# Gate and up of two row blocks made together by seven half products, and two turns moved to TensorE

## The chip, the core and the metric

The kernel runs on one core of one Trainium2 chip. A core has a matrix engine (TensorE, PE in the profile, with its weight loads as PEld), a vector engine (VectorE, DVE), a scalar engine (ScalarE, ACT), a general engine (GpSimd, POOL) and a queue engine (SyncE, SP) that here issues every transfer between DRAM and the on-chip memory. PE writes into eight banks of 128 x 512 floats; DVE and ACT read them. The metric is the time of one execution in microseconds of device time.

## The reference

One pre-norm transformer block on 2048 rows of 640 numbers, in float32.

```python
def _A_ref(x, wqkv, wo):          # H = 32 heads of 20, window W = 8, dilation 2
    qkv = (x @ wqkv).reshape(B, S, 3, H, Dh) ...
    idx = pos[:, None] - off[None, :]          # each row looks at 8 rows, 2 apart
    logits = einsum("bhsd,bhswd->bhsw", q, k[idx]) * scale
    o = einsum("bhsw,bhswd->bhsd", softmax(logits), v[idx])
    return o.reshape(B, S, D) @ wo

def _B_ref(x, w_gate, w_up, w_down):           # 640 -> 1728 -> 640
    return (_silu(x @ w_gate) * (x @ w_up)) @ w_down

h  = x + _A_ref(_layernorm(x), wqkv, wo)
h2 = h + _B_ref(_layernorm(h), w_gate, w_up, w_down)
```

## The kernel before

**Tiles.** The 2048 rows are four blocks (0 to 3) of 512; a block lies on 128 partitions as four row groups j. The 640 columns are five chunks of 128 (c = 0 to 4). The 1728 hidden columns are 14 tiles (0 to 13) of 128, the last of 64. Attention runs on DVE by block and by four head groups of 8 heads.

**Three passes.** A float32 number is kept as a rounded high half and the rest, a low half. ACT casts the high half and DVE subtracts to get the low one. A product is three passes: high x high, high x low, low x high. So gate and up of one tile in one block are 2 x 5 chunks x 3 passes = 30 matmuls (`proj`, L756), into banks 5 and 6; ACT then makes the SiLU of the gate's bank (L787), DVE multiplies it with the up bank (L788), and ACT and DVE split the result (L789, L791). The down product (`down`, L768) adds it into banks 0 to 4, five banks x 3 passes = 15 matmuls a tile. `finish` turns bank 4 with four transposes (L813) and adds the banks to the residual rows.

**Stages on PE.** First the qkv products of all blocks (`qkv`, L515), then the output projection of block 0 (`wo`, L686) and its norm; then, for each block, 14 tiles of gate, up and down, with the next block's output projection and norm strewn in between (bank 7). Attention on DVE runs beside all of this until block 2's tiles, and its results go over DRAM (`osc`) back as columns, in four transfers per half block and head group.

**The norm between the projection and gate/up.** Its rows have to be turned into columns. Block 0 does so on PE (`x_columns`, five times four transposes, L408, with high half on ACT L411 and low half on DVE L412). Blocks 1 and 2 turn half by DVE and DRAM and half on PE (`pair_columns`). Block 3 turns all rows by DVE and DRAM (`turn_rows`, `turned_back`, `turned_columns`), since it is in `TURN`.

**Weights.** `load_ffn` brings a tile's gate, up and down weights (960 KB, L732) into one of two raw buffers. In block 0 the low halves are made on DVE (L750) and stored in DRAM (`lsc`); blocks 1 and 2 load them from there (`LOADED`, L738); block 3 makes them again on DVE.

**What sets the order.** The functions only add operations to a plan, with the ranges that each reads and writes, an assumed cost and a priority. `Plan.order` places them by a list schedule on the five engines (smaller priority number first among those that are ready), shifts a few operations by a table that is keyed by an operation's number (`SHIFT`), and writes the program out in that order. Each engine then runs its own queue strictly in order; a wait in front of an instruction holds all that is behind it, on SP too.

Of the kernel before, what the change touches and what calls it, by code (L numbers as in the profile page):

```python
# [23 lines left out]
NF = 14  # L24
KEPT = range(NF)
LOADED = (1, 2)
TURN = (3,)
# [7 lines left out]
PR = {'x': 4, 'yst': 8, 'yld': 6, 'wqd': 1.5, 'wqh': 8, 'wql': 2.5, 'qev': 0.5, 'kvs': 4, 'atl': 0.9, 'exp': 0.9, 'ost': 0.9, 'wod': 4, 'woh': 8, 'wol': 2.5, 'old': 1, 'fld': 2.5, 'lst': 10, 'wev': 2.5, 'fh': 1.2, 'fl': 0.5, 'ln1': 10, 't1': 3, 'wo0': 0.4, 'wo': 2, 'ln1t': 8, 'xb': 0.4, 'tr': 1.2, 't1t': 6, 'ln1d': 1.5, 'hst': 1, 'hld': 6, 'ht': 3, 'hc': 0.4}  # L35
# [111 lines left out]
tt = dve  # L147
# [10 lines left out]
def program(tc, x_in, wqkv_in, wo_in, ffn_in, ffl_in, const_in, out):  # L158
# [7 lines left out]
    with tc.tile_pool(name="sb", bufs=1) as sb, tc.tile_pool(  # L166
# [6 lines left out]

        def sha_t():
            if "sha" not in late:
                late["sha"] = sb.tile([128, 5120], F32R, name="sha", tag="sha")
            return late["sha"]

        def h_t():
            if "h" not in late:  # L180
                late["h"] = sb.tile([128, 5120], F32, name="h", tag="sha")
            return late["h"]
# [19 lines left out]
        zsc = dr.tile([NB, D, 4, 64], F32, name="zsc")  # L202
        lsc = dr.tile([NF, 128, 1920], F32, name="lsc")
# [58 lines left out]
        class LnStats:  # L262
# [41 lines left out]
            def apply_pair(self, j):  # L304
                o = lambda: f(XN, 1280).rearrange("p (f j t) -> p f j t", j=2, t=32)[:, :, j, :]
                P.add("ACT", 0.95, lambda: A.activation(o(), self.src(j).rearrange("p (f t) -> p f t", t=32), AF.Identity, bias=f(self.NB + j, 1), scale=f(self.RS + j, 1)),
                      r=[self.srcr(j), rf(self.NB + j, 1), rf(self.RS + j, 1)], w=[rf(XN, 1280)], prio=self.prio)

# [273 lines left out]

        def att_av(b, g, n, ko, vo, qo, lo, mo):
# [7 lines left out]
            for jp in range(2):  # L591
# [11 lines left out]
                for m in (4, 2):  # L603
                    P.add("DVE", tt(320 * m), lambda m=m, half=half: half(m, lambda v: v[:, :, 0:m, :]),
                          r=[rf(PROD, 2560)], w=[rf(PROD, 2560)], prio=20)
                P.add("DVE", tt(320), lambda half=half: half(1, lambda v: v[:, :, 0:1, :]), r=[rf(PROD, 2560)], w=[rf(PROD, 2560)], prio=20)
# [26 lines left out]
        def hsl(b, j, o=0, n=640):  # L633
            s = 2560 * (b % 2) + 640 * j + o
            return s, s + n

        wn = [0]
        ln = [0]

        def wo(b, prio, bks):  # L640
# [16 lines left out]
            stats = LnStats(b, lambda j: h_t()[:, slice(*hsl(b, j))], lambda j: ("sha",) + hsl(b, j), prio, turned=b in TURN)  # L657
            h0 = 2560 * (b % 2)
            if b:
                P.add("SP", 0.6, lambda: Q.dma_start(h_t()[:, h0 : h0 + 2560], x_in[b].rearrange("p j c -> p (j c)")),  # L660
                      w=[("sha", h0, h0 + 2560)], prio=PR["old"], nbytes=nb(512, 2560))
            for j in range(NJ):
# [3 lines left out]
                for i in range(3) if j % 2 == 0 else ():  # L666
# [11 lines left out]
                for half in range(2):  # L678
# [10 lines left out]
                    P.add("ACT", act(320), lambda bk=bk, xo=xo: A.copy(f(xo, 320), banks[bk][:, 0:320]), r=[pb(bk)], w=[rf(xo, 320)], prio=PR["wev"])  # L689
                lo, hi = hsl(b, j)  # L690
                if b:
                    P.add("DVE", dve(640), lambda lo=lo, hi=hi, j=j: V.tensor_add(h_t()[:, lo:hi], h_t()[:, lo:hi], f(XN + 640 * j, 640)),
                          r=[rf(XN + 640 * j, 640), ("sha", lo, hi)], w=[("sha", lo, hi)], prio=prio)
                else:
                    xr = XR + 640 * (j % 2)
                    P.add("SP", 0.45, lambda j=j, xr=xr: Q.dma_start(f(xr, 640), x_in[0, :, j, :]), w=[rf(xr, 640)], prio=PR["old"], nbytes=nb(128, 2560))
                    P.add("DVE", dve(640), lambda lo=lo, hi=hi, j=j, xr=xr: V.tensor_add(h_t()[:, lo:hi], f(xr, 640), f(XN + 640 * j, 640)),
                          r=[rf(XN + 640 * j, 640), rf(xr, 640)], w=[("sha", 0, 5120) if j == 0 else ("sha", lo, hi)], prio=prio)
                stats.one(j)
# [9 lines left out]
                if b == 0 and j >= NJ - 2:  # L709
# [4 lines left out]
            if b and b not in HALF:  # L714
# [45 lines left out]
        def down(i, ao, dn, k):  # L760
            first, last = i == 0, i == NF - 1
            passes = ((0, 0), (0, 1)) if last else ((0, 0), (1, 0), (0, 1))
# [187 lines left out]
```

## Time and profile before

| | us |
|---|---|
| median of the three runs shown | 860.32 |
| lowest and highest | 858.07, 860.82 |
| the profiled execution, its own time | 857.67 |
| its span | 855.9 |

The profile has one execution. Its page lists busy times by engine, then the span in 40 slices of 21.4 us, where a digit is the busy share in tenths. A list of waits says who waited for whom: the total, how often, the longest. Rows in order of time give the start, the length, the engine, the line, the operation, what it writes and reads, and the number of instructions merged in the row; in brackets stands the idle time before it and what ended it. The end of a matmul is modelled and reaches into the next one, so distances are taken from start to start.

In the trace, block 1's tiles begin at 399.11 us, block 2's at 556.87 us and block 3's at 713.38 us; attention's last row on DVE begins at 614.31 us; PE's last matmul ends at about 852.3 us.

### The profile page before, as it was taken

The numbers are of one execution on the slowest core, as the hardware profiler recorded it, in microseconds if no ns is written. First come the engines' busy times: TensorE is split into PE (matmuls) and PEld (weight loads), VectorE is DVE, ScalarE is ACT, GpSimd is POOL, SyncE is SP. The second block draws the span as 40 slices with busy tenths as digits, with TensorE's granted clock in tenths as the row PEclk, the third lists the DMA queues.
The fourth block names the chain that finished last, engine by engine and source line by source line (L and its number), as shares of the span: only waits on it lengthen the run. The fifth ranks groups of instructions, "written<-read, shape, count | busy, mean of one in ns | idle before, by whom it ended". The sixth has DMA issues, their size and how long they took to land.

```text
span 855.9 us, 10646 instructions
## 1 busy us (share of the span) xinstructions
PE 848.7 (99%) x3987; PEld 721.3 (84%) x3987; DVE 658.4 (77%) x781; ACT 395.7 (46%) x637; POOL 2.5 (0%) x10
## 2 busy tenths in 40 slices
PE   9999999999999999999999999999999999999998
PEld 7888888889878888988888898888888888888886
DVE  7799999999999999999999998999622326333332
ACT  7571463434763334666434468444355534333321
POOL 0000000000000000000000000000000000000000
PEclk9999999999999999999999999999999999999999
DMA  8998697579786969398999976897552755222301
GB/s 285 278 296 252 199 275 205 155 212 293 235 265 243 291 223 311 128 242 276 316 309 322 287 233 205 241 360 273 180 204 94 227 203 200 92 93 93 105 18 62
DMA packets 87732, 187.90 MB, mean 220 GB/s; under 512 B 34289, under 2 KB 51185, under 8 KB 86913
## 3 DMA queue, kind: packets, MB, share of 16 engines
q1 hardware_dynamic: 87680, 187.23, 68.6%
q8 instruction: 31, 0.51, 0.2%
q14 instruction: 21, 0.16, 0.1%
HBM read 142.23 MB, written 44.96 MB: 219 GB/s over the span
## 4 chain that ended last, share of the span: by engine, by line
PE 71%; DVE 18%; DMA 6%; issue 3%; ACT 1%; SPq 0%; DVEq 0%; ACTq 0%
PE bank L756 43%; PE bank L768 22%; PE bank L686 6%; DVE fa L594 4%; DVE fa L602 4%; DVE fa L563 2%; DVE fa L568 2%; DMA fa<-in_x_dram 1%; DMA fa<-qsc 1%; DMA qsc<-st 1%; DVE ra L491 1%; DMA osc<-fa 1%; DVE fa L316 1%; DVE fa L609 1%; DMA fa<-in_const_dram 1%
## 5 line engine op out<-in xcount | busy, mean ns | idle before, releaser
L756 PE MATMUL bank<-shb,ra 128*128 128x512 f32 x1620 | 379.7, 390 | 1.3 <-DVE shb L412 1.3
L756 PEld LDWEIGHTS bank<-shb,ra 128*128 128x128 f32 x1620 | 303.1, 188 | 63.5 <-ACT shb L411 1.5
L768 PE MATMUL bank<-ra,acts 128*128 128x512 f32 x656 | 160.6, 390 | 0.0
L768 PEld LDWEIGHTS bank<-ra,acts 128*128 128x128 f32 x656 | 122.5, 188 | 25.0
L788 DVE TENSOR_TENSOR fa<-bank,fa 128x512 f32<-128x512 f32 x52 | 35.9, 690 | 113.4 <-PE bank L756 113.0
L515 PE MATMUL bank<-ra,sha 128*128 128x480 f32 x480 | 106.1, 380 | 0.5 <-ACT sha L478 0.3
L515 PE MATMUL bank<-ra,shb 128*128 128x480 f32 x470 | 102.9, 378 | 0.1
L515 PEld LDWEIGHTS bank<-ra,sha 128*128 128x128 f32 x480 | 89.8, 188 | 14.4 <-ACT sha L478 0.6
L515 PEld LDWEIGHTS bank<-ra,shb 128*128 128x128 f32 x470 | 88.0, 188 | 13.6 <-DVE shb L398 0.4
L733 ACT CAST ra<-fa 128x1280 fp32r<-128x1280 f32 (+1 forms) x56 | 68.9, 1230 | 58.7 <-PE bank L756 58.5
L594 DVE TENSOR_TENSOR fa<-fa 128x1280 f32<-128x1280 f32 x64 | 93.6, 1488 | 1.0
L563 DVE TENSOR_TENSOR fa<-fa 128x2560 f32<-128x2560 f32 x32 | 90.3, 2821 | 1.8 <-DMA fa<-qsc 1.4
L602 DVE TENSOR_TENSOR fa<-fa 128x1280 f32<-128x1280 f32 (+2 forms) x96 | 89.7, 934 | 2.5
L568 DVE TENSOR_REDUCE fa<-fa 128x128 f32<-128x2560 f32 x32 | 90.0, 2814 | 0.4
L787 ACT ACTIVATE fa<-bank 128x512 f32<-128x512 f32 x52 | 31.1, 599 | 104.9 <-PE bank L756 101.3
L750 DVE TENSOR_TENSOR ra<-fa,ra 128x640 fp32r<-128x640 f32 (+1 forms) x82 | 64.6, 818 | 18.1 <-ACT ra L734 18.0
L520 ACT ACTIVATE st<-bank,fa 128x480 f32<-128x480 f32 x64 | 42.0, 658 | 76.4 <-PE bank L515 74.8
L686 PE MATMUL bank<-ra 128*128 128x320 f32 x480 | 74.8, 309 | 0.5 <-DVE ra L676 0.5
L686 PEld LDWEIGHTS bank<-ra 128*128 128x128 f32 x480 | 72.4, 188 | 2.8 <-DVE ra L676 0.7
L734 ACT CAST ra<-fa 128x640 fp32r<-128x640 f32 x56 | 40.8, 730 | 59.6 <-PE bank L768 59.6
L789 ACT CAST acts<-fa 128x512 fp32r<-128x512 f32 x52 | 32.2, 619 | 43.1 <-DVE fa L788 40.4
L768 PE MATMUL bank<-acts,ra 128*128 128x512 f32 x164 | 46.2, 390 | 0.0
(101 smaller groups left out, 487.7 us busy)
## 6 DMA issues: line engine op xcount, KB each, us to landing
fa<-in_ffn_dram SPq DMA_DIRECT2D x52, 960.0 KB, 6.6
ra<-lsc SPq DMA_DIRECT2D x26, 640.0 KB, 5.6
fa<-ksc SPq DMA_DIRECT2D x32, 440.0 KB, 5.9
fa<-vsc SPq DMA_DIRECT2D x32, 440.0 KB, 6.6
ra<-lsc SPq DMA_DIRECT2D x30, 320.0 KB, 4.9
lsc<-ra SPq DMA_DIRECT2D x13, 640.0 KB, 5.7
ksc<-st SPq DMA_DIRECT2D x32, 160.0 KB, 3.9
qsc<-st SPq DMA_DIRECT2D x16, 320.0 KB, 5.0
```

Source lines behind the costliest of these rows:

```text
L515: T.matmul(banks[bk][:, 0:480], l, r_(wq(g, w, c), 480), start=(p, c) == first_mm, stop=(p, c) == last_mm)
L520: P.add("ACT", act(480) + 0.06, lambda bk=bk, j=j: A.activation(stage_t()[:, so : so + 1920].rearrange("p (t j c) -> p t j c", t=3, j=NJ)[ ...
L563: P.add("DVE", dve(2560), lambda: V.tensor_tensor(f(PROD, 2560).rearrange("p (j w c) -> p j w c", j=2, w=W), window(ko, 2 * jp), f(qo + 32 ...
L568: P.add("DVE", dve(2560), lambda: V.tensor_reduce(f(lo + 128 * jp, 128), f(PROD, 2560).rearrange("p (n d) -> p n d", d=DH), axis=AX.X, op= ...
L594: V.tensor_tensor(f(PROD + 1280 * jj, 1280).rearrange("p (w h d) -> p w h d", w=W, d=DH), f(vo + 160 * j, 1280).rearrange("p (w h d) -> p ...
L602: V.tensor_add(dst(v), v[:, :, 0:m, :], v[:, :, m : 2 * m, :])
L686: T.matmul(banks[bk][:, 0:320], l, r_(m, 320), start=p == 0 and c == 0, stop=p == 2 and c == NC - 1)
L733: P.add("ACT", act(n), lambda: A.copy(r_(gu, n), f(raw, n)), r=[rf(raw, n)], w=[rr(gu, n)], prio=PR["fh"])
L734: P.add("ACT", act(640), lambda: A.copy(r_(dn[0], 640), f(raw + n, 640)), r=[rf(raw + n, 640)], w=[rr(dn[0], 640)], prio=PR["fh"])
L750: P.add(eng, c, lambda o=o: E.tensor_sub(ra[p0:, lo + o : lo + o + 640], fa[p0:, raw + o : raw + o + 640], ra[p0:, hi + o : hi + o + 640]. ...
L756: T.matmul(banks[bk], r_(gu + 1280 * w + wid * c + col, 128), x2(a, c), start=p == 0 and c == 0, stop=p == 2 and c == NC - 1)
L768: T.matmul(banks[k], l, m, start=first and p == 0, stop=last and p == len(passes) - 1)
```

## The change

**Seven half products.** Take tiles p and p + 6 (p = 0 to 5) as one pair, and blocks 2 and 3. Of the five chunks, 0 and 1 are one half of the columns and 2 and 3 the other; chunk 4 is done plainly. With A11, A12 the halves of block 2's normed columns, A21, A22 those of block 3, and B11, B21 the weights of tile p, B12, B22 those of tile p + 6, the four products of block and tile are made by Winograd's form of Strassen's scheme, from column sums S1 = A21 + A22, S2 = S1 - A11, S3 = A11 - A21, S4 = A12 - S2 and weight sums T1 = B12 - B11, T2 = B22 - T1, T3 = B22 - B12, T4 = B21 - T2 (the last with its sign turned):

- A11 B11 and A12 B21 are made early (`early`), as part of block 2's tile p, which is then finished as before. The first of the two is copied from its bank by ACT before the second is added, and stored in DRAM (`msc`), for gate and for up.
- S2 T2, S1 T1, S3 T3, A22 T4 and S4 B22 are made later (`pair`), for gate and up, on banks 5, 6 and 7. The running sums are read from a bank by DVE while its accumulation goes on.
- A pair gives tile p and tile p + 6 of block 3 at once, and tile p + 6 of block 2, whose gated product is kept in on-chip memory; its down products run at the very end (`closing`).

So the order of stages behind block 1 is: tiles 12 and 13 of block 2, six early tiles, the output projection and norm of block 3, tiles 12 and 13 of block 3, six pairs, block 3's rows out, six closing down products for block 2, its rows out. The column sums are made once by DVE and ACT (`column_combinations`), the weight sums for each pair (`combo`).

**Turns.** The norm of block 3 is turned on PE (20 transposes) as block 0's, its statistics are made on DVE, and ACT keeps the sorted columns in float32 too, since the sums need them. The last head group of block 3 is no longer turned by DVE and sent over DRAM: PE turns it (two times four transposes, `last_columns`), and only the three groups before it come from DRAM. Block 2's down sum is added to its rows in two parts, so `finish` turns a bank once more (four transposes).

Some priorities change too. The table of shifts keeps its numbers, which count operations, so from the first added operation on they mean other ones. Parts of the diff that only rename or resize buffers are left out below.

```diff
-TURN = (3,)
+TURN = ()
...
+        def last_columns(jp, at, col, sorted_, prio):
...
+            def tr():
+                for jj in range(2):
+                    for t, s in ((0, -96), (1, 32)):
+                        T.transpose(banks[bk][:, 256 * jj + 128 * t : 256 * jj + 128 * t + 128], f(last_rows(2 * jp + jj) + s, 128), ident)
...
+        def product(bk, terms, start, stop):
+            for p, (w, a) in enumerate(((0, 0), (0, 1), (1, 0))):
...
+        def early(p):
...
+            load_ffn(2, p, gu, dn)
+            ws = lambda c, col: (gu + 256 * c + col, gu + 1280 + 256 * c + col)
+            both = ((5, 0), (6, 128))
+            for n, (bk, col) in enumerate(both):
+                product(bk, [(ws(0, col), x2, (0, 1), shr)], True, False)
+                P.add("ACT", act(512), lambda n=n, bk=bk: A.copy(f(EB[n], 512), banks[bk]), ...)
+                P.add("SP", 0.45, lambda n=n: Q.dma_start(msc[p, n], f(EB[n], 512)), ...)
+            for bk, col in both:
+                product(bk, [(ws(2, col), x2, (2, 3, 4), shr)], False, True)
+            gate(p, ao, so, JG)
...
+        def pair(p):
+            lo_, hi_ = RAW, RAW + 1920
...
+            t1 = combo(1, 0, B12, B11)
+            t2 = combo(0, 1, B22, t(0))
+            t3 = combo(2, 2, B22, B12)
+            t4 = combo(3, 3, B21, t(1))
...
+            X, Y = (5, 7), (6, 5)
+            def add(h, bk, src, dst):
+                dv(0, lambda: V.tensor_add(fb(h, dst), banks[bk], fb(h, src)), ...)
+            def sum_of(h, part):
+                if part == 0:
+                    product(X[h], [(t2(C[h]), c2, (0, 1), c2r)], True, False)
+                    add(h, X[h], 0, 1)
+                elif part == 1:
+                    product(Y[h], [(t1(C[h]), c1, (0, 1), c1r), (kws(1, C[h]), x3, (4,), x3r)], True, False)
+                elif part == 2:
+                    product(X[h], [(t3(C[h]), c3, (0, 1), c3r)], False, False)
+                    add(h, X[h], 0, 2)
+                elif part == 3:
+                    product(X[h], [(t4(C[h]), x3, (2, 3), x3r), (kws(0, C[h]), x3, (4,), x3r)], False, True)
+                    add(h, X[h], 0, 0)
+                elif part == 4:
+                    add(h, Y[h], 2, 2)
+                else:
+                    product(Y[h], [(b22(C[h]), c4, (0, 1), c4r), (kws(1, C[h]), ck, (0,), ckr)], False, True)
+                    add(h, Y[h], 1, 1)
+            for n, (h, part) in enumerate(((0, 0), (0, 1), (1, 0), (0, 2), (0, 4), (1, 2), (0, 3), (1, 3), (0, 5), (1, 1), (1, 4), (1, 5))):
...
-        for b in range(NB):
-            if b + 1 < NB:
-                wo(b + 1, PR["wo"], (7,))
...
+        for b in range(2):
+            wo(b + 1, PR["wo"], (7,))
             do_down = ffn(b)
-            if b + 1 < NB:
-                ln2_columns(b + 1, 1)
+            ln2_columns(b + 1, 1)
             do_down()
             finish(b)
...
+        for i in range(2 * NP, NF):
+            step(plain(i, x2, shr))
+        for p in range(NP):
+            step(early(p), 2 if p == NP - 1 else 1)
+        wo(3, PR["w3"], (7,))
+        ln2_columns(3, 1)
...
+        finish(2, store=False)
+        column_combinations()
...
+        for i in range(2 * NP, NF):
+            step(plain(i, x3, x3r))
+        for p in range(NP):
+            for t in pair(p):
+                step(t)
+        downs([pend.pop(0)], False, True)
+        finish(3)
...
+        downs(todo, False, True, fb)
+        finish(2, fb, final=True)
```

How the queues change is shown at three places. In these rows bank_73, 74 and 75 are banks 5, 6 and 7, and bank_68 to 72 banks 0 to 4.

PE's queue before, one tile of block 2 or 3 in its steady state: gate, up, then the down product of the tile before (L756 is `proj`, L768 `down`).

```order
L756 MATMUL bank_73<-shb,ra 128x512 x15
L756 MATMUL bank_74<-shb,ra 128x512 x15
L768 MATMUL bank_72<-acts,ra 128x512 x3
L768 MATMUL bank_68<-ra,acts 128x512 x3
L768 MATMUL bank_69<-ra,acts 128x512 x3
L768 MATMUL bank_70<-ra,acts 128x512 x3
L768 MATMUL bank_71<-ra,acts 128x512 x3
```

PE's queue now, one pair (L932 is `product`, L857 `down`); in the order of the rows: S2 T2 of the gate, S1 T1 of the gate, S2 T2 of up, S3 T3 of the gate and of up, A22 T4 of the gate and of up, S4 B22 of the gate, S1 T1 of up, down products, S4 B22 of up.

```order
L932 MATMUL bank_73<-ra 128x512 x6
L932 MATMUL bank_74<-ra 128x512 x9
L932 MATMUL bank_75<-ra 128x512 x6
L932 MATMUL bank_73<-shb,ra 128x512 x6
L932 MATMUL bank_75<-shb,ra 128x512 x6
L932 MATMUL bank_73<-ra 128x512 x9
L932 MATMUL bank_75<-ra 128x512 x9
L932 MATMUL bank_74<-shb,ra 128x512 x9
L932 MATMUL bank_73<-ra 128x512 x9
L857 MATMUL bank_72<-acts,ra 128x512 x3
L857 MATMUL bank_68<-ra,acts 128x512 x3
L932 MATMUL bank_73<-shb,ra 128x512 x9
```

Two products on the same bank now stand 6 matmuls apart at three points (bank 5 from its S3 T3 to its A22 T4, bank 7 from its S2 T2 to its S3 T3, bank 5 from up's S1 T1 to its S4 B22), with a read by DVE between; before, a bank's next product stood 30 matmuls on.

DVE's queue now, from the start of the column sums to tile 13's gated product (L993 to L1000 the sums, L992 their low halves, L872, L876, L883 and L878 the gated products of block 3's tiles 12 and 13 and their low halves).

```order
L993 TENSOR_TENSOR fa<-fa 128x1024
L995 TENSOR_TENSOR fa<-fa,shb 128x1024
L996 TENSOR_TENSOR fa<-fa,shb 128x1024
L998 TENSOR_TENSOR fa<-shb,fa 128x1024
L872 TENSOR_TENSOR fa<-bank_74,fa 128x512
L992 TENSOR_TENSOR ra<-fa,ra 128x1024
L883 TENSOR_TENSOR acts<-fa,acts 128x512
L992 TENSOR_TENSOR ra<-fa,ra 128x1024
L999 TENSOR_TENSOR fa<-fa,shb 128x1024
L876 TENSOR_TENSOR fa<-bank_73,fa 64x512
L1000 TENSOR_TENSOR fa<-shb,fa 128x1024
L878 TENSOR_TENSOR acts<-fa,acts 64x512
```

Behind these come the last two sums, the four weight sums of pair 0, their low halves, and the first two reads of pair 0's banks, before the low half of S3.

SP's queue now, around the first weights of pair 0 (L1024 the two raw tiles, L1018 the low half of down weights, L828 low halves of block 3's tiles 12 and 13, L970 and L1028 the stored products out and in).

```order
L822 DMA fa<-in_ffl_dram 128x1280
L1028 DMA fa<-msc 128x512
L828 DMA ra<-lsc 128x1280
L970 DMA msc<-fa 128x512 x2
L1018 DMA ra<-lsc 128x640
L828 DMA ra<-lsc 128x640
L1024 DMA fa<-in_ffn_dram 128x1920
L828 DMA ra<-lsc 128x640 x2
L1024 DMA fa<-in_ffn_dram 128x1920
```

The L828 row ahead of the first raw tile goes into a place that the down weights of the last early tile hold, so the raw tile is issued when that tile's down products are done.

More of the change, by code (lines that the diff above doesn't have):

```diff
@@ L172, in program, with __init__, __getitem__, two @@
         late = {}
+        class Two:
+            def __init__(self, *t):
+                self.t = t
+            def __getitem__(self, at):
+                o = 2560 * (at[1].start >= 2560)
+                return self.t[o // 2560][:, at[1].start - o : at[1].stop - o]
+        def two(name, dtype):
+            if name not in late:
+                late[name] = Two(*(sb.tile([128, 2560], dtype, name=f"{name}{i}", tag=f"sha{i}") for i in range(2)))
+            return late[name]
         def sha_t():
[L175 to L177 removed]
+            return two("sha", F32R)
         def h_t():
[L180 to L182 removed]
+            return two("h", F32)
+        def upper(name, dtype):
+            if name not in late:
+                late[name] = sb.tile([128, 2560], dtype, name=name, tag="sha1")
+            return late[name]
         def stage_t():
@@ L665, in wo @@
                 jp = j // 2
-                for i in range(3) if j % 2 == 0 else ():
+                if b == 3 and j % 2 == 0:
+                    last_columns(jp, at, col, sorted_, prio)
+                for i in range(3) if j % 2 == 0 and b < 3 else ():
                     c, n = 2 * i, 1 if i == 2 else 2
@@ L767, in down, with downs @@
                     l, m = act_t()[:, ao + 512 * a + 128 * k : ao + 512 * a + 128 * k + 128], r_(dn[w], 512)
-                T.matmul(banks[k], l, m, start=first and p == 0, stop=last and p == len(passes) - 1)
+                T.matmul(banks[bk], l, m, start=first and p == 0, stop=last and p == len(passes) - 1)
+        DB = (0, 1, 2, 3, 4)
+        def downs(batch, first, last, db=DB):
+            for k in (4, 0, 1, 2, 3):
+                P.add("PE", sum(3 if t[0] < NF - 1 else 2 for t in batch) * 0.229,
+                      lambda k=k: [down(*t, k, first and n == 0, last and n == len(batch) - 1, db[k]) for n, t in enumerate(batch)],
+                      r=[x for i, ao, dn in batch for x in (("ab", ao, ao + 1024), rr(dn[0], 640), rr(dn[1], 640))], w=[pb(db[k])], prio=10)
@@ L770, in ffn, with halves, do_down @@
+        def halves(src, srcr, ao, prio=0, lprio=0):
+            P.add("ACT", act(512), lambda: A.copy(act_t()[:, ao : ao + 512], src()), r=srcr, w=[("ab", ao, ao + 512)], prio=prio)
+            P.add("DVE", dve(512), lambda: V.tensor_sub(act_t()[:, ao + 512 : ao + 1024], src(), act_t()[:, ao : ao + 512].bitcast(F32)),
+                  r=srcr + [("ab", ao, ao + 512)], w=[("ab", ao + 512, ao + 1024)], prio=lprio)
         def ffn(b):
             pend = []
-            def do_down(count=1):
-                batch = [pend.pop(0) for _ in range(count)]
-                for k in (4, 0, 1, 2, 3):
-                    P.add("PE", sum(3 if t[0] < NF - 1 else 2 for t in batch) * 0.229,
-                          lambda k=k: [down(i, ao, dn, k) for i, ao, dn in batch],
-                          r=[x for i, ao, dn in batch for x in (("ab", ao, ao + 1024), rr(dn[0], 640), rr(dn[1], 640))], w=[pb(k)], prio=10)
+            def do_down():
+                t = pend.pop(0)
+                downs([t], t[0] == 0, t[0] == NF - 1)
@@ L821, in finish @@
                     if j == 0:
[L822 to L825 removed]
+                        keys = [hrow(b, k, 512, 128)[1] for k in range(NJ)]
```

326 lines of the change are left out of this document (273 added, 53 removed).

## The prediction

> **What bounds the kernel now.** I read the page's busy times, slices and chain first, then what the matmul engine waited for, then its rows in order of time.
>
> ```profile
> span 855.9 us, 10646 instructions
> PE 848.7 (99%) x3987; PEld 721.3 (84%) x3987; DVE 658.4 (77%) x781; ACT 395.7 (46%) x637; POOL 2.5 (0%) x10
> PE   9999999999999999999999999999999999999998
> DVE  7799999999999999999999998999622326333332
> PEclk9999999999999999999999999999999999999999
> PE 71%; DVE 18%; DMA 6%; issue 3%; ACT 1%; SPq 0%; DVEq 0%; ACTq 0%
> ```
>
> TensorE (PE) is busy in every slice; VectorE (DVE) is full for the first two thirds only, and in the last stage has more than half its time free:
>
> ```profile
> 697.00:856.00 159.00, 155.33 (x690) 128.26 (x688) 61.96 (x89) 50.62 (x67) 0.63 (x1) 1.00 0.27 95
> ```
>
> (a row of the windows: stretch, length, busy time of PE, weight loads, DVE, ACT and POOL, granted clock, DMA's share, GB/s). The waits of PE, added up, say how little a better order could still give:
>
> ```profile
> PE bank L423 <- POOL ra L842: 1.3, 1, 1.3
> PE bank L756 <- DVE shb L412: 1.3, 1, 1.3
> PE bank L686 <- DVE ra L676: 0.5, 1, 0.5
> PE bank L515 <- ACT sha L478: 0.3, 1, 0.3
> PE bank L515 <- ACT ra L489: 0.2, 1, 0.2
> ```
>
> That is 3.6 us in 855.9. So the time is the number of matmuls by what each takes, and a matmul taken out is time taken out, until something makes PE wait. What one takes is read from the distance between rows in order of time, since the last matmul of a row overlaps the next row:
>
> ```profile
> 533.87 0.60 PE L373 MATMUL bank<-fa 128*128 128x128 f32 x4
> 534.23 2.33 PE L768 MATMUL bank<-ra,acts 128*128 128x512 f32 x9
> 556.87 13.80 PE L756 MATMUL bank<-shb,ra 128*128 128x512 f32 x60
> 594.31 6.96 PE L756 MATMUL bank<-shb,ra 128*128 128x512 f32 x30
> 601.11 0.84 PE L768 MATMUL bank<-acts,ra 128*128 128x512 f32 x3
> 628.31 2.36 PE L686 MATMUL bank<-ra 128*128 128x320 f32 x15
> 630.50 1.32 PE L756 MATMUL bank<-shb,ra 128*128 128x512 f32 x5
> ```
>
> Thirty matmuls of 512 columns take 601.11 - 594.31 = 6.80 us, 0.2267 us each; four transposes of 128x128 take 0.36 us, 0.09 each; fifteen of the output projection's 320-column matmuls 2.19 us. Block 2's feed-forward part starts at 556.87 us, and up to there PE's queue stays as it was but for two or three pieces moved by a few places.
>
> **Matmuls out and in.** A pair of column tiles in two blocks was 2 x 2 x 2 (gate, up) x 5 chunks x 3 passes = 120 matmuls. Now the early part has 30, and the seven half products' rest 2 x (2 + 3 + 2 + 3 + 3) x 3 = 78, so 108: twelve fewer in each of six pairs, 72, at 0.2267 us: **-16.3 us**. Added are 32 transposes: 20 for block 3's norm, 8 for the last head group, 4 because block 2's down sum is now turned and added twice: 32 x 0.09 = **+2.9 us**. Nothing else on PE changes in number. What is left is where PE waits.
>
> By the Trainium skill (TensorE: Matmul & The Clock Gate, section on the clock gate) a warm matmul comes every N / 2.4 GHz + 2.5 ns, 215.7 ns at 512 columns, by which the 72 would be 15.5 us. The trace's 226.7 is used.
>
> **Place 1: block 3's norm comes back through PE.** Before, it was turned by DVE and DRAM, far from PE. Now the last row group's chain (copy, sum, statistics, root, scale, transposes, halves) ends directly before the first block-3 tile. The nearest row is block 0, which does the same already:
>
> ```profile
> 239.01 1.04 PE L408 MATMUL bank<-fa 128*128 128x128 f32 x8
> 239.77 1.06 ACT L411 CAST shb<-bank 128x512 fp32r<-128x512 f32 x2
> 240.49 1.88 DVE L412 TENSOR_TENSOR shb<-bank,shb 128x512 fp32r<-128x512 f32 x3
> 241.32 13.85 PE L756 MATMUL bank<-shb,ra 128*128 128x512 f32 x60 [1.27 <-DVE shb L412]
> ```
>
> PE stood 1.27 us after its transposes. Between the last transposes and the first block-3 product there are now three down matmuls (0.7 us) as cover, and two more casts on ScalarE (ACT) ahead (the sorted copies of the norm, 0.6 each). These cancel about: **+1.3 us**; bounds 0 and 3.
>
> **Place 2: from the first block-3 tile to the first pair's third half product.** This is the dearest term. Here DVE makes the four combinations of normed columns and the four of weights, and PE has only tiles 12 and 13 of block 3 to do meanwhile. DVE's rates:
>
> ```profile
> 557.75 1.87 DVE L820 TENSOR_TENSOR h<-bank,h 128x512 f32<-128x512 f32 x3
> 573.39 2.89 DVE L594 TENSOR_TENSOR fa<-fa 128x1280 f32<-128x1280 f32 x2
> 590.91 0.84 PE L768 MATMUL bank<-acts,ra 128*128 128x512 f32 x3
> 591.18 0.69 DVE L788 TENSOR_TENSOR fa<-bank,fa 128x512 f32<-128x512 f32 x1 [1.12 <-PE bank L756]
> 591.78 2.81 DVE L568 TENSOR_REDUCE fa<-fa 128x128 f32<-128x2560 f32 x1
> ```
>
> 512 elements alone take 0.69 us but follow each other every 0.60; 1280 every 1.40, so 1024 some 1.13 (on the line between). From the last low half of block 3's columns to the low half of the third combination (first read in pair 0's third half product) DVE's queue holds 10 operations of 1024 and 17 of 512: 11.3 + 10.2 = 21.5 us, 23.9 if none overlaps. PE's queue has 88 matmuls between the same points: 19.9 us. So PE waits 1.6 to 4.0 us even if DVE never does. DVE will wait once: its queue is strict, and the gated product of tile 12 stands in it behind ACT's SiLU, which stands behind two casts of pair 0's weights. Their transfer is queued on SP behind a load into tile 13's slot that the last early tile's down matmuls hold, and so starts about when the first block-3 tile does:
>
> ```profile
> fa<-in_ffn_dram SPq DMA_DIRECT2D x11, 960.0 KB, 6.3
> fa<-in_ffn_dram SPq DMA_DIRECT2D x11, 960.0 KB, 4.7
> 243.27 1.28 ACT L787 ACT_TABLE_LOAD   x1
> ```
>
> (before's windows 560 to 700 and 700 to 850 us). Landing at 4.7 to 6.3, two casts 1.1, table load 1.3, SiLU 0.6: 7.7 to 9.3 us after the tile's start, where DVE would otherwise have come to that product at about 7 (30 matmuls 6.8, and 0.27 from PE to DVE as in the rows at 590.91 and 591.18). Late by 0.7 to 2.3. Together 2.3 to 6.3; I take **+4.5 us**, above the middle because each late operand also holds matmuls that the next one waits for.
>
> **Place 3: inside the pairs.** A running sum is read from its bank and the next half product is added onto the same bank, with 6 matmuls in between at three points of a pair: 6 x 0.2267 = 1.36 us. The trip is 0.27 (PE's next row to DVE's start) + 0.69 + some 0.15 back (an estimate, half of the 0.27) = 1.1 us. It fits when DVE is free, and in the order it is at two of the three; at the third (before up's last product) two 512-operations run ahead and still end in time. DVE has 21 such operations in a pair, 12.6 to 14.5 us of its 108 x 0.2267 = 24.5. Taken as **0**; if one more DVE operation (0.60) stands ahead at each point, 0.34 us x 18 = 6.2 us.
>
> The Trainium skill (Perfetto Trace Analysis, Optimizing Tensor Performance, Matmuls) says that matmul groups should rotate through banks so that one's evacuation overlaps the next's matmuls, which these sums do over three banks only; it is the rule behind the second rival below.
>
> **Place 4: small ones.** PE must find the last attention group's columns ready at the output projection of block 3: 253 matmuls and four transposes after 556.87, plus nine more, 616.6 us. Attention's last DVE rows in this trace:
>
> ```profile
> 613.79 0.49 DVE L602 TENSOR_TENSOR fa<-fa 128x320 f32<-128x320 f32 x1
> 614.31 0.51 DVE L609 STREAM_TRANSPOSE fa<-fa 128x320 f32<-128x320 f32 x1
> ```
>
> The last transpose goes, and three column halves (0.60 + 0.60 + 0.35) come ahead and two (0.8) behind: about 616 us, half a microsecond before PE asks. The early tiles' bank copies on ACT (0.60 and the two trips, 1.0 us, under 1.36 or, once, 0.68) two gated products asked for early, and one pass in block 1 that now comes 12 matmuls sooner and so meets the read of its bank, cost some tenths each. **+1.0 us**, bounds 0 and 3.
>
> **Place 5: transfers in the pairs.** Both raw weight tiles have one buffer each. The second is free after the pair's second product and a copy (some 5.6 us into the pair), and its next use is DVE's first combination for the next pair, some 13 us in, with 0.8 us of further slack before a matmul is late: 8 us for a transfer that took 4.7 to 6.6. **0**; the other end is the first rival's.
>
> **Sum** on the profiled execution (857.67 us, of them 855.9 span): -16.3 + 2.9 + 1.3 + 4.5 + 1.0 = -6.6, so 851.1. The median of the runs shown, 860.32, is 2.65 above that execution, so **853.7 us** as the runs go.
>
> **Rivals.**
> (a) Late weights, the other side. Each pair's combinations stand in DVE's strict queue ahead of the reads that free the banks, so a tile landing after its 8 us holds PE one for one, in five pair changes. For it: 3.7 MB (raw tiles 1.97, low halves and stored products 1.70) go through one queue in each pair, in strict order behind its waits, and one kind took longer than that where the queue was full:
>
> ```profile
> out_dram<-h SPq DMA_DIRECT2D x2, 320.0 KB, 11.8
> ```
>
> Against it: in the last stage DMA was busy 27% at 95 GB/s, and a pair asks for 150 GB/s (3.7 MB in 24.5 us). With landing at 11.8: 5 x 3.8 = 19 us, 872.7. It decides from 8 + 6.6 / 5 = 9.3 us on.
> (b) Bank trips exposed: Place 3's 6.2 us and Place 2's upper end (+1.8): 853.7 + 8.0 = 861.7, no measurable change. For it: PE issues in strict order and nothing else can fill in. Against: the three operations ahead of each read are counted above. If a wait passed some 3.4 us, by the Trainium skill (the same TensorE page and section) the clock would halve for such a window, +1.7 us; here the granted clock stayed at 1.00 with waits up to 1.3.
> (c) Full gain: the waits of Places 1, 2 and 4 vanish under what PE has queued: -13.4, 846.9. Against: DVE's 21.5 us against 19.9 is a count.
>
> **How the numbers follow.** Forecast 0.62, (c) 0.14, (b) 0.13, (a) 0.11. About 0.3% (2.6 us) is what a measurement here tells from no change. Forecast and (c), with a little of (b)'s lower part, are faster: 0.78. The rest of (b): same, 0.11. (a): slower, 0.11. The range runs from (c), 847, to 861: Places 1, 2 and 4 at their ends give -6.6 + 5.5 = -1.1, 859.2, and most of (b) is taken in.
>
> **What would show it.** In the changed kernel PE's 512-column matmuls number 2379 and the transposes 128. Steady pairs should be 24.5 us apart, with no PE wait over 0.3 us in them (Place 3, 5). PE's waits should sit between the last transposes and the first pair, on DVE's combinations and gated products, 4 to 8 us in all. It is wrong if the pairs are 26 us apart or more (a, b), if that stretch costs under 2 or over 10 us, or if PE waits for the last attention columns by more than 2 us.

## The result, and the profile after

| | before | changed |
|---|---|---|
| median of four runs beside each other, us | 860.13 | 851.73 |
| lowest and highest | 858.07, 860.82 | 851.40, 852.59 |
| the profiled execution, its time and span | 857.67, 855.9 | 851.40, 849.6 |

The ratio is 0.9908 (95% interval 0.9889 to 0.9927), and 0.9924 (0.9911 to 0.9938) in a second set of runs: about 0.8 to 0.9% faster. The prediction was 853.7 us, within 847 to 861; on the profiled execution it was -6.6 us, and -6.3 came. The median came 2.0 us lower than predicted because the 2.65 us between profiled execution and median, taken over from the kernel before, were not there: the changed kernel's median lies 0.3 us above its profiled execution.

The page of the changed kernel: span, busy times of TensorE and of VectorE, the 40 slices of VectorE, the granted clock of TensorE (in tenths of full speed; 9 is 90% or more).

```profile
span 849.6 us, 10832 instructions
PE 839.5 (99%) x3947; PEld 709.9 (84%) x3947; DVE 719.4 (85%) x892; ACT 403.3 (47%) x669; POOL 1.9 (0%) x9
DVE  7799999999999999999999899999945986555652
PEclk9999999999999999999999999999999999999999
```

PE is as full as before over a shorter span. DVE is nearly full once more in the two slices from 658 to 701 us (9 and 8 tenths), where the column sums are made, and then about half busy to the last slice but one, where it mostly had a third or less. From the list of PE's waits, longest in total first:

```profile
...
PE bank L857 <- DVE acts L878: 0.9, 2, 0.8
PE bank L932 <- ACT ra L1048: 0.9, 1, 0.9
...
PE bank L932 <- DVE shb L992: 0.3, 1, 0.3
PE bank L846 <- DVE fa L872: 0.2, 1, 0.2
PE bank L846 <- ACT fa L871: 0.2, 1, 0.2
```

These five were not there before: tile 13's low half (L878, in block 2 and in block 3), the cast of a weight sum (L1048), the low half of a column sum (L992), and two short ones in block 1 (L871, L872). A bank read of the pairs (L1070) or a transfer is not among them. The pairs themselves, in order of time (start, length, operation, number of matmuls): the first rows of pairs 2, 3 and 4.

```profile
722.95 4.92 PE L932 MATMUL bank<-ra 128*128 128x512 f32 x21
...
747.43 4.92 PE L932 MATMUL bank<-ra 128*128 128x512 f32 x21
...
771.91 4.92 PE L932 MATMUL bank<-ra 128*128 128x512 f32 x21
```

They are 24.48 us apart, as is pair 5 from pair 4: 108 x 0.2267 = 24.48. What was lost was lost between block 3's first tile and pair 1, which begins at 698.47:

```profile
658.23 10.49 PE L954 MATMUL bank<-ra 128*128 128x512 f32 x45
...
672.89 0.74 PE L857 MATMUL bank<-acts,ra 128*128 128x512 f32 x2 [0.77 <-DVE acts L878]
...
676.34 5.08 PE L932 MATMUL bank<-ra 128*128 128x512 f32 x21 [0.85 <-ACT ra L1048]
...
682.14 2.56 PE L932 MATMUL bank<-shb,ra 128*128 128x512 f32 x10 [0.27 <-DVE shb L992]
```

698.47 - 658.23 = 40.24 us for 163 matmuls, which are 36.95: **3.3 us**. These 40.24 us are called the stretch below. Up to the wait in the third half product, for which 4.5 us were predicted, it is 682.14 - 658.23 = 23.91 us for 93 matmuls, which are 21.08: 2.8 us. The prediction's forecast of 4 to 8 us of waiting between the last transposes and the first pair was too high. A second loss lies where only some tenths had been costed, in block 1. Its first tile begins at 399.37 us, block 2's at 558.16: 158.79 us, where the kernel before took 157.76 (399.11 to 556.87).

### The profile page after: what moved, and what is told of

Same layout as the page of the kernel before. It is cut to its first block, busy times and chain, and to the rows that moved or that the text cites. A ratio compares the mean times of both kernels' runs of the same rounds, so it can differ in the third digit from the quotient of the medians.

```text
span 849.6 us, 10832 instructions
## 1 busy us (share of the span) xinstructions
PE 839.5 (99%) x3947; PEld 709.9 (84%) x3947; DVE 719.4 (85%) x892; ACT 403.3 (47%) x669; POOL 1.9 (0%) x9
## 5 line engine op out<-in xcount | busy, mean ns | idle before, releaser
L846 PE MATMUL bank<-shb,ra 128*128 128x512 f32 x810 | 191.3, 390 | 1.7 <-DVE shb L441 1.3
L846 PEld LDWEIGHTS bank<-shb,ra 128*128 128x128 f32 x810 | 151.2, 188 | 33.5 <-ACT shb L440 1.5
L857 PE MATMUL bank<-ra,acts 128*128 128x512 f32 x656 | 162.8, 391 | 0.0
L857 PEld LDWEIGHTS bank<-ra,acts 128*128 128x128 f32 x656 | 122.1, 188 | 24.7
L932 PE MATMUL bank<-shb,ra 128*128 128x512 f32 x360 | 87.6, 391 | 0.3 <-DVE shb L992 0.3
L932 PEld LDWEIGHTS bank<-shb,ra 128*128 128x128 f32 x360 | 67.0, 188 | 15.2 <-ACT fa L969 0.7
L1070 DVE TENSOR_TENSOR fa<-bank,fa 128x512 f32<-128x512 f32 x60 | 41.1, 691 | 44.3 <-PE bank L932 43.2
L776 PEld LDWEIGHTS bank<-ra 128*128 128x128 f32 x480 | 72.0, 188 | 3.8 <-ACT fa L779 1.0
L932 PE MATMUL bank<-ra 128*128 128x512 f32 x288 | 68.5, 390 | 0.9 <-ACT ra L1048 0.9
L932 PEld LDWEIGHTS bank<-ra 128*128 128x128 f32 x288 | 53.9, 188 | 12.9 <-ACT ra L1048 1.3
L823 ACT CAST ra<-fa 128x1280 fp32r<-128x1280 f32 (+1 forms) x38 | 46.0, 1211 | 28.6 <-PE bank L846 23.5
L882 ACT CAST acts<-fa 128x512 fp32r<-128x512 f32 x47 | 29.2, 620 | 50.1 <-DVE fa L1100 22.9
```

Of the source, the lines that this page charges most:

```text
L776: T.matmul(banks[bk][:, 0:320], l, r_(m, 320), start=p == 0 and c == 0, stop=p == 2 and c == NC - 1)
L823: P.add("ACT", act(n), lambda: A.copy(r_(gu, n), f(raw, n)), r=[rf(raw, n)], w=[rr(gu, n)], prio=PR["fh"])
L846: T.matmul(banks[bk], r_(gu + 1280 * w + wid * c + col, 128), x2(a, c), start=p == 0 and c == 0, stop=p == 2 and c == NC - 1)
L857: T.matmul(banks[bk], l, m, start=first and p == 0, stop=last and p == len(passes) - 1)
L932: T.matmul(banks[bk], r_(ws[w] + 256 * q, 128), x(a, c), start=start and p == n == q == 0, stop=stop and p == 2 and n == len(terms) - 1 an ...
L1070: dv(0, lambda: V.tensor_add(fb(h, dst), banks[bk], fb(h, src)), [pb(bk)] + fr(h, src), fr(h, dst))
```

## The experiments

All are compared with the kernel before on the same chip; the changed kernel ran once more beside the first three.

> The changed kernel as it is, a yardstick for the runs beside it: 851.7 us (851.4 to 852.6 so far), block 2's first tile at 558.2 us and pairs 24.48 us apart in its profile.

851.84 us (850.83 to 854.34) against 858.72. Block 1 took 158.79 us again.

### The table of shifts put right

```diff
-    22: -2, 28: 8, 104: 3, 554: 8, 576: -0.5, 674: -1, 1039: -1, 1109: -6, 1110: -4, 1111: -4, 1223: -2, 1540: -2,
-    1623: -17, 1632: -1, 1637: 2, 1643: -4, 1712: -16, 1720: -15, 1938: -8, 1943: 2, 2058: 6
+    22: -2, 28: 8, 104: 3, 554: 8, 576: -0.5, 674: -1, 1031: -1, 1101: -6, 1102: -4, 1103: -4, 1215: -2, 1532: -2,
+    1615: -17, 1624: -1, 1629: 2, 1635: -4, 1704: -16, 1712: -15
```

> The changed kernel with the table of shifts put right: each key from 1039 to 1720 lowered by 8, so that it means the operation it meant before, and the last three keys dropped. Theory: the 1.0 us by which block 2 starts later than before (beside 0.27 in the first microsecond) comes from the two passes of block 1 that the stale keys moved; so block 2's first tile at 557.2 us in place of 558.2, and 0.8 to 1.2 us less in all, 850.7. Rival: the block 1 rows are late for another reason (new priorities, other transfers) and the moved passes cost nothing: block 2 still at 558.2, 851.7.

851.08 us against 858.72, ratio 0.9913 (0.9901 to 0.9926); a second set on another chip, 850.56 against 858.27, 0.9909 (0.9894 to 0.9924).

> The kernel with the table of shifts put right once more, beside the next one: 7.6 us under the kernel before (851.08 against 858.72 in its first runs). Its first profile had a stretch at a lower granted clock (0.71 at 160 to 164 us, behind a wait of 0.86 us); if that was this one execution's, block 0's first tile is at 241 to 242 us here in place of 243.8, and block 2's first tile at 557.2; if it comes with this order of transfers, it is there again.

The medians lie 0.8 and 1.3 us below the changed kernel's 851.84, a difference that the intervals alone would not carry. The trace does. Block 1 in the changed kernel, then in the second run of this one:

```profile
436.13 0.84 PE L857 MATMUL bank<-ra,acts 128*128 128x512 f32 x3
437.18 7.09 PE L846 MATMUL bank<-shb,ra 128*128 128x512 f32 x30 [0.21 <-ACT fa L871]
...
474.71 0.84 PE L857 MATMUL bank<-acts,ra 128*128 128x512 f32 x3
475.78 1.43 PE L846 MATMUL bank<-shb,ra 128*128 128x512 f32 x5 [0.23 <-DVE fa L872]
```

```profile
437.22 0.84 PE L857 MATMUL bank<-ra,acts 128*128 128x512 f32 x3
437.90 6.96 PE L846 MATMUL bank<-shb,ra 128*128 128x512 f32 x30
...
475.30 0.84 PE L857 MATMUL bank<-acts,ra 128*128 128x512 f32 x3
475.98 2.88 PE L857 MATMUL bank<-ra,acts 128*128 128x512 f32 x12
```

Three matmuls of a down product take 0.68 us to the next row in the second kernel; in the changed one they take 1.05 and 1.07, each time with gate or up of the next tile asked for before its bank had been read. With the table right, block 1 takes 157.76 us in both profiles (400.46 to 558.22 in the second), the figure of the kernel before to the hundredth, and block 2 up to block 3's first tile 99.52 in place of 100.07. So the stale keys cost **1.0 us in block 1 and 0.55 in block 2**; the rival falls. What lies ahead of block 0's first tile varies between executions (its start lies between 240.95 and 245.33 us in the twelve profiles), which hides a part of it in the medians.

### The turn alone

```diff
-TURN = (3,)
+TURN = ()
...
-... 1938: -8, 1943: 2, 2058: 6
+... 1932: -8, 1937: 2, 2052: 6
```

(in the kernel before; nothing else of the change)

> The kernel before with block 3's norm turned on TensorE and nothing else of the change (the last three keys of the shift table lowered by 6 so that they mean the same operations). It makes 20 more transposes and the whole norm of block 3. By the prediction: 20 x 0.09 = 1.8 us of transposes and 1.3 of waiting, +3.1: 863.2, with PE's wait on the low half of the columns at 1 us or more. By the changed kernel's trace: each group of four transposes costs 0.46 and not 0.36, five groups 2.3, and a wait of 0 to 0.3, +2.3 to +2.6: 862.6. Rival: the turn over DRAM that is removed had held something up, and nothing is lost: 860.1.

861.09 us against 858.72, ratio 1.0028 (1.0016 to 1.0039): +2.4. From block 2's first tile to block 3's it took 158.89 us (557.84 to 716.73), where the kernel before took 156.51 (556.87 to 713.38): +2.38, and no wait of PE in it. Three rows in order of time:

```profile
668.58 0.60 PE L408 MATMUL bank<-fa 128*128 128x128 f32 x4
668.93 2.56 PE L756 MATMUL bank<-shb,ra 128*128 128x512 f32 x10
671.33 0.84 PE L768 MATMUL bank<-acts,ra 128*128 128x512 f32 x3
```

The four transposes take 0.35, but the ten matmuls behind them 2.40 where ten take 2.27: a group of transposes costs about 0.12 us more than its own 0.36, at the change to the wide matmuls. Five groups at 0.48 are 2.40, beside the measured 2.38. So the turn is paid for in full, by its transposes and their changes and not by a wait. The 1.3 us of waiting that the prediction gave it did not come here, but here the last transposes (711.53) stand 5.2 us ahead of block 3's first tile, so this run does not test it. Nor did it come in the changed kernel, where the last transposes are followed by three down matmuls and then, 0.78 us later, by block 3's first tile at 658.23 without a wait.

### Three pairs

```diff
-        NP = 6
+        NP = 3
```

> The changed kernel with three pairs in place of six (tiles p and p + 3; tiles 6 to 13 plain). Theory A, the sum: 3 x 12 matmuls more, 36 x 0.2267 = 8.2 us; and since eight plain tiles of block 3 now stand before the first pair in place of two, the 3.3 us of waiting between block 3's first tile and pair 1 fall to 0.5 or less. 851.7 + 8.2 - 2.8 = 857.1. Rival B: the waits there go with each start of pairs, whatever stands before it: 859.9. Rival C: the pairs save less than their matmuls, since the last stage has other limits: under 855.

857.73 us against 858.72, ratio 0.9989 (0.9979 to 0.9999); 5.9 above the changed kernel beside it, with 5.4 expected by A and 8 by B. The pairs' first rows, and no wait between them:

```profile
766.57 4.92 PE L932 MATMUL bank<-ra 128*128 128x512 f32 x21
...
789.92 4.92 PE L932 MATMUL bank<-ra 128*128 128x512 f32 x21
...
814.40 4.92 PE L932 MATMUL bank<-ra 128*128 128x512 f32 x21
```

Pairs 1 and 2 are 24.48 us apart again; pair 0, with eight plain tiles in place of two ahead of it, runs without the waits of the stretch (23.35 us, since five of its matmuls stand elsewhere). So a pair saves its twelve matmuls, 2.72 us, and the stretch's loss belongs to the short cover ahead of pair 0, not to pairs as such. B and C fall. The result is half a microsecond over A; PE has waits of 1.0, 0.9 and 0.7 us here that the changed kernel doesn't have, two on loads and one on a bank copy, which is more than enough for it.

### DVE's work in the stretch, less and more

In the changed kernel, `put`, where the low half of a column sum is made (0 times or 2 times for the first three sums):

```diff
-lambda: V.tensor_sub(dst(1, m), f(at_(n), m), dst(0, m).bitcast(F32))
+lambda: [V.tensor_sub(dst(1, m), f(at_(n), m), dst(0, m).bitcast(F32)) for _ in range(0 if n in (0, 1, 2) else 1)]
```

> The changed kernel without the low halves of the first three column combinations (C1, C2, C3; three DVE operations of 1024 elements, so the products with them use what stood there before; every other instruction keeps its place). Theory, DVE bounds the stretch from block 3's first tile to pair 0's third half product: DVE has 3 x 1.2 = 3.6 us less there, 19.0 us beside PE's 19.9, so the 3.3 us by which that stretch (to pair 1's start) is longer than its matmuls falls to 1 or less: 849.4, 2.3 us below the changed kernel. Rival, pair 0's weights or ACT's casts bound it: the stretch stays within 0.7 us, 851.2.

> The changed kernel with the same three DVE operations made twice, one behind the other. Theory: one for one, 3 x 1.2 = +3.6 us in that stretch, 855.4. Rival: hidden behind the weights or ACT, at most +1, 852.8.

Twice: 855.51 us against 858.73 (ratio 0.9959, 0.9945 to 0.9974), +3.7 on the changed kernel, and the stretch 44.03 us (663.10 to 707.13), +3.8: one for one, with the wait on L878 grown from 0.8 to 2.7 us and that on L992 from 0.3 to 1.5. Left out: by the median, 851.72 us (850.23 to 852.20), nothing is gained, but its interval (ratio 0.9902 to 0.9933) is too wide to tell 0.7 from 2.3 us. In the profile the stretch is 38.80 us (658.52 to 697.32), 1.44 less, where the theory had 2.3 at least and the rival 0.7 at most: it lies between the two. One wait stayed as it was:

```profile
675.89 5.10 PE L932 MATMUL bank<-ra 128*128 128x512 f32 x21 [0.90 <-ACT ra L1048]
```

So more work on DVE costs its full time, but less work does not give its full time back. With two low halves gone ahead of them, DVE comes to the gated products of tiles 12 and 13 before ACT has made their operands, and waits 1.44 us:

```profile
667.13 0.69 DVE L883 TENSOR_TENSOR acts<-fa,acts 128x512 fp32r<-128x512 f32 x1 [0.69 <-ACT acts L882]
...
669.71 0.69 DVE L876 TENSOR_TENSOR fa<-bank,fa 64x512 f32<-64x512 f32 x1 [0.75 <-ACT fa L875]
```

Pair 0's first half product then waits for the cast of a weight sum as before. In the changed kernel DVE and ACT make it as follows:

```profile
674.61 2.01 DVE L1047 TENSOR_TENSOR fa<-fa 128x512 f32<-128x512 f32 x3
...
674.72 1.05 ACT L991 CAST shb<-fa 128x1024 fp32r<-128x1024 f32 x1 [2.07 <-DVE fa L1002]
675.67 1.66 ACT L1048 CAST ra<-fa 128x512 fp32r<-128x512 f32 x3
```

The first of the three sums, 0.68 us, is done at 675.29; its cast starts 0.38 us later, behind the cast of the third column sum. That is less than half of the 0.85 us that PE waits. The rest is the weight sum's own place in DVE's queue, behind the column sums. By DVE's rows this wait adds nothing by itself in the changed kernel: DVE works without a break from 658.27 to the end of the third sum's low half (682.09), for which PE has to wait in any case.

### The bank reads of a pair made twice

```diff
-dv(0, lambda: V.tensor_add(fb(h, dst), banks[bk], fb(h, src)), ...)
+dv(0, lambda: [V.tensor_add(fb(h, dst), banks[bk], fb(h, src)) for _ in range(2 if src != dst else 1)], ...)
```

> The changed kernel with four of each pair's six to eight bank reads on DVE made twice (the sums of the first and the third half product, for gate and up), one 512-element operation more ahead of the bank's next matmul. By the prediction's Place 3 (a trip of 1.1 us beside 6 matmuls, 1.36 us, and 0.60 for one more operation) PE would wait 0.34 us at the two points of a pair that have 6 matmuls between, 0.7 a pair: pairs 25.2 us apart in place of 24.48, and in pair 0, where DVE is late already, up to 1.2 more; +4 to +5, 856.2. Rival A: the trip is shorter than 0.76 us, and pairs stay at 24.48: under 853. Rival B: DVE has no room in the pairs and each of the four costs its 0.60: 2.4 a pair, +14, 866.

856.72 us (ratio 0.9984, 0.9973 to 0.9995), +4.9. Pairs are 25.0 us apart (700.93, 725.97, 750.98, 775.98), and the stretch is 2.2 longer. In pair 2:

```profile
730.73 1.52 PE L932 MATMUL bank<-shb,ra 128*128 128x512 f32 x6
732.40 1.65 PE L932 MATMUL bank<-shb,ra 128*128 128x512 f32 x6
733.89 4.33 PE L932 MATMUL bank<-ra 128*128 128x512 f32 x18
```

Six matmuls, 1.36 us, are followed after 1.67 and 1.49: 0.31 and 0.13 lost, where 0.34 was expected at each. So the trip with one operation more is 1.67, and without it 1.67 - 0.60 = 1.07 (1.1 predicted). Place 3 was zero by a margin of 0.3 us, half of one more DVE operation.

### The weights of the pairs later

```diff
-lambda i=i, raw=raw: Q.dma_start(f(raw, 1920), ffn_in[i])
+lambda i=i, raw=raw: [Q.dma_start(f(raw, 1920), ffn_in[i]) for _ in range(2 if p else 1)]
```

> The changed kernel with each raw weight tile of pairs 1 to 5 (960 KB) loaded twice in a row into its buffer, so that it is there later. Its loads landed after 5.8 us (4.7 to 7.7) so far. Theory (Place 5): 8 us of slack from the second tile's issue; twice the bytes land after 8 to 12 us, so PE waits 0 to 4 us in each of five pair changes, +0 to +20, and the time follows the landing: 5 x (landing - 8) us. Rival: the slack is longer than counted, since the combinations can be late without PE being late, and nothing is seen up to 10 us of landing: 851.7.

883.92 us (ratio 1.0295, 1.0271 to 1.0319): +32, more than either. The second load of a tile goes out only when the first has landed. DVE's first weight sum for pair 3, made during pair 2, and PE's rows of pair 2:

```profile
757.90 0.69 DVE L1047 TENSOR_TENSOR fa<-fa 128x512 f32<-128x512 f32 x1 [5.40 <-DMA fa<-in_ffn_dram]
```

```profile
739.25 4.92 PE L932 MATMUL bank<-ra 128*128 128x512 f32 x21
...
761.05 3.82 PE L932 MATMUL bank<-shb,ra 128*128 128x512 f32 x9 [4.64 <-DVE fa L1070]
764.71 2.23 PE L857 MATMUL bank<-ra,acts 128*128 128x512 f32 x9
```

In the changed kernel the same sum runs 13.16 us into the pair (736.11 - 722.95); here 18.65 (757.90 - 739.25). It is 5.49 us late. PE's row behind the wait starts 21.80 us into the pair (761.05 - 739.25) in place of 17.00 (739.95 - 722.95), 4.80 late: beyond the sum there were 0.7 us of slack, where the prediction had 0.8. From the second tile's issue (728.31 in the changed kernel) to that sum are 7.8, so 8.5 us in all against the 8 predicted; the rival falls. The landing here took 11.9 us (745.97 to 757.90), counted from the first issue, which itself came 1.4 us later in the pair. PE waited 18.7 us in four of the pair changes and 4.0 in the other. The rest of the 32 is in the row behind the wait: nine matmuls took 3.66 us (761.05 to 764.71) and not 2.04. The windows of another pair change (stretch, length, PE and the others busy, granted clock, DMA's share, GB/s) show why:

```profile
819.00:822.00 3.00, 0.26 (x1) 0.26 (x2) 2.96 (x6) 1.56 (x3) 0.00 (x0) 1.00 0.01 3
822.00:825.00 3.00, 3.00 (x9) 2.33 (x9) 2.21 (x4) 1.84 (x3) 0.00 (x0) 0.55 0.00 0
```

After a wait of 3.63 us the granted clock was 0.55 for the next 3 us. That cost 1.5 to 1.8 us at each of the five pair changes, some 8 in all, which with the 22.7 of waiting is nearly the 32.

### The sums in another order

On the kernel with the table put right: a second table gives 31 operations a time of their own in the plan, between 677 and 694 us (operation number: time in the plan), and nothing is left out.

```diff
+AT = {2183: 677.2, 2215: 677.5, 2231: 677.9, 2216: 677.95, 2232: 678.3, 2217: 678.5, 2234: 679.0, ...}
...
-        key = [(t + SHIFT.get(n, 0.0), n) for n, t in enumerate(start)]
+        key = [(AT.get(n, t + SHIFT.get(n, 0.0)), n) for n, t in enumerate(start)]
```

> The shift table put right, and DVE's and ACT's order between block 3's first tile and pair 0 written out: the chunk 4 sum's first step, tile 13's gated product and its low half, and pair 0's first two weight sums go ahead of the third and fourth column sum; the end of the fourth, of chunk 4's and pair 0's last weight sum go behind the third's low half. The same operations, none left out; TensorE's order is unchanged. Theory: of the 3.3 us between block 3's first tile and pair 1, 0.77 is tile 13's low half standing behind the sums, 0.85 the cast of a weight sum standing behind the cast of the third column sum (it stayed when three low halves were left out, which took 1.4 us off), 0.27 the third's low half; in the new order each of them is ready before TensorE asks, so 2 to 2.5 us less than the kernel with the table put right, that stretch 38.0 in place of 40.2. Rival: the stretch is bound by the sum of DVE's work and no order helps: the wait moves to another operand of pair 0, under 0.7 us gained.

848.16 us against 858.27, ratio 0.9884 (0.9870 to 0.9897); 2.4 us under the kernel with the table put right beside it. Its interval lies below that of the changed kernel's second set (from 0.9911) and overlaps by a little that of the kernel beside it (from 0.9894), so the trace has to carry the rest. The stretch is 38.49 us (656.69 to 695.18) in place of 40.28 (657.74 to 698.02). PE's rows in it:

```profile
670.46 0.61 PE L857 MATMUL bank<-acts,ra 128*128 128x512 f32 x2
...
672.72 4.92 PE L932 MATMUL bank<-ra 128*128 128x512 f32 x21
677.48 1.56 PE L932 MATMUL bank<-shb,ra 128*128 128x512 f32 x6
680.08 1.66 PE L932 MATMUL bank<-shb,ra 128*128 128x512 f32 x6 [1.04 <-DVE fa L1070]
```

The waits on tile 13's low half and on the cast are gone, and that on the third column sum too. One of 1.04 us is new: a bank read of pair 0 now stands behind a step of the fourth column sum (1.22 us) in DVE's queue. The low half of the third sum is done 19.7 us after the last low half of block 3's columns (658.01 to 677.69), in place of 22.6. So 1.8 of the 3.3 us were order, a little less than the 2 to 2.5 expected, and the rival falls in the main, though it has a part: some of the work is only moved to where PE meets it next. This is the fastest kernel of the study, 1.2% under the kernel before.

## Why the prediction was right, and where it was not

- **Matmuls, -16.3.** Right. The count is 2379 matmuls of 512 columns as predicted, the pairs are 24.48 us apart, and half the pairs give half the saving.
- **Transposes, +2.9.** Too small. The step "32 x 0.09" counted the transposes and not the change behind them: 0.12 us for each group of four as the run with the turn alone has it, eight groups, **1.0 us more** (an estimate for the three groups that this run does not have).
- **Place 1, +1.3.** Wrong: no wait before the first tile. The step "these cancel about" failed. The two sorted copies (L1164) on ACT cost nothing, since they ran beside the transposes, and of the columns only two low halves were left to make:

```profile
656.23 1.04 ACT L1164 COPY fa<-bank 128x512 f32<-128x512 f32 x2
656.65 1.04 PE L437 MATMUL bank<-fa 128*128 128x128 f32 x8
657.29 1.08 ACT L440 CAST ra<-bank 128x512 fp32r<-128x512 f32 x2
658.27 1.27 DVE L441 TENSOR_TENSOR ra<-bank,ra 128x512 fp32r<-128x512 f32 x2
```

  From the transposes to the end of the last low half are 2.89 us here, and 3.36 in the prediction's rows of block 0 (239.01 to 242.37), which have a third low half. Of block 0's wait of 1.27 that leaves 0.8, and the three down matmuls cover 0.78. This is worked out from the rows; no run tests it by itself. By chance the term was near what the changes of the line above cost.
- **Place 2, +4.5.** The mechanism was right and its size 1.2 too large: 3.3 over the whole stretch. DVE's count was right; from the last low half of block 3's columns to that of the third sum (659.5 to 682.1 us) it took 22.6 us, within 21.5 to 23.9, without a wait. The part of 0.7 to 2.3 us for late weights did not come. I had the first raw tile queued behind a load that waits for the last early tile. The trace has it ahead:

```profile
653.68 0.32 SPq L828 DMA_DIRECT2D ra<-lsc  x1
654.21 0.33 SPq L1024 DMA_DIRECT2D fa<-in_ffn_dram  x1
...
659.23 0.33 SPq L1024 DMA_DIRECT2D fa<-in_ffn_dram  x1
```

  It left 4 us before block 3's first tile. The load at 653.68 went out 0.2 us after the last early tile's down products began (653.49), so it had waited for the tile before that one, and not for the last as the section on the change has it. Tile 12's gated product on DVE (665.44) then came when DVE got to it, 2.4 us after ACT's SiLU was done. What the prediction lacked is that DVE's order could be better: the count of 27 operations is fixed only for this order, and with some of them behind the third sum's low half the stretch is 1.8 us shorter.
- **Place 3, 0.** Right, by 0.3 us.
- **Place 4, +1.0.** Half right. The last attention columns were in time: the transposes at 616.24 us and the projection at 618.75 follow without a wait. The projection was worked out for 616.6; of the 2.1 us more, 1.3 are block 2's later start. But the passes moved by stale keys, put at "some tenths", cost 1.0 in block 1 and 0.55 in block 2.
- **Place 5, 0.** Right: 8.5 us of slack, and landings of 4.7 to 7.7.

Put against the stages: the kernel is 0.26 us later at block 1's first tile, loses 1.03 in block 1, and is 7.59 shorter from there on (291.44 us against 299.03). In that last part -16.3 + 2.9 + 1.0 + 0.55 + 3.3 leave 1.0 us. Some 0.2 of it is at the end, behind the last transposes; the rest is spread over small delays among block 2's tiles and projections, of which the profile marks one (0.16 us), and its cause stays open. So the sum came out right to 0.3 us because two terms were 2.5 too large (Place 1 by 1.3, Place 2 by 1.2) and others 2.8 too small or left out (the changes behind transposes 1.0, the stale keys beyond Place 4's 1.0 another 0.55, 0.26 ahead of block 1, 1.0 in small delays). That agreement is luck; what held is the saving in matmuls, and that each place stayed within its bounds.

Of the rivals, (a) decides where it was said to: with a landing near 12 us PE waits 3.6 to 5.9 us at a pair change. It was dearer than its 5 x 3.8 since the waits add up to 22.7 us and each also halved the clock. (b) needed one more operation ahead of each read; with one at two of the three points the time was 856.7, and here there was none. (c) is nearly reached once the table is put right and the sums are reordered: 848.2 against its 846.9.

## What to carry to other kernels

A matmul taken out of a queue that is full is time taken out, and pays as counted as long as each new operand has its cover; the loss sits where two stages meet and the second one's operands are all made at once, so count each engine's queue there, ACT's too, and order it by what the consumer asks for first. A table that moves work by its number has to be moved with the numbers: here that was 1.6 us beside a gain of 7 to 8. When a zero is predicted, measure its margin: 0.3 us at the banks and about 3 at the weights (8.5 of slack, 5.8 the median landing; under 1 beside the longest, 7.7) were very different zeros.

## What the runs showed of the hardware

- A group of four 128x128 transposes delays the matmuls of 512 columns behind it by 0.12 us, beside its own 0.36 (turn alone: 2.38 us for five groups, no wait).
- After waits of 3.6 to 5.9 us PE came back at a granted clock of 0.50 to 0.55 for some 3 us (nine matmuls in 3.5 to 3.9 us in place of 2.04); after waits of 2.7 and 1.5 us it stayed at 1.00. That agrees with the Trainium skill (TensorE: Matmul & The Clock Gate, section on the clock gate), by which an idle window of about 3.4 us halves it.
- In two of the twelve profiles the clock fell after a far shorter wait. In the first profile of the kernel with the table put right PE waited 0.86 us up to 156.38, and in that of the low halves made twice 1.38 us up to 157.90. Here are 156 to 164 us of the first (stretch, length, PE's busy time, granted clock, DMA's share, GB/s); in the second the clock was 0.57 from 160 to 164 us.

```profile
156.00:160.00 4.00, 3.15 (x7) 0.87 0.88 268
160.00:164.00 4.00, 4.00 (x15) 0.71 0.06 17
```

  Matmuls had become sparse before it: 7 and 5 from 156 to 160 us, where twenty fit. The one with the weights loaded twice had 11 there and a wait of 0.52 us, and its clock stayed at 1.00. Beside it block 0's projection begins 1.8 us later in the first profile (197.39 against 195.62) and 3.3 later in the second (198.91), whose execution took 860.05 us where the median is 855.51. In the profiles of the kernel before, of the changed one and of the second run with the table put right PE waited 1.3 us ahead of block 0, and the clock stayed at 1.00 there. What made it fall in the two is open.
